# Backward attention in groups of eight units: the query gradient's products three units later, the row jobs in units 2 to 4, the key and value sums in units 5 and 6, nine E buffers

## The chip, the cores and the metric

The kernel runs on one core of one Trainium2 chip. The metric is the device time of one execution in microseconds (us). The kernel before has a median of 1660.38 us over 3 runs (1658.82 to 1664.07). One execution was also profiled; its durations are those used below.

## The reference

One transformer block with a parallel sum, forward and backward, for one sequence of S = 2048 rows and D = 448 columns, H = 16 heads of 28, and a feed-forward width of F = 1792, all in bfloat16:

```
xn  = (x - mean(x)) / sqrt(var(x) + 1e-5)
qkv = xn @ wqkv                     # split into q, k, v; 16 heads of 28
p   = softmax(q @ k.T * 28**-0.5)
out = x + (p @ v) @ wo + (silu(xn @ w_gate) * (xn @ w_up)) @ w_down
```

The outputs are `out` and the gradients, for a given `grad_out`, of `x`, `wqkv`, `wo`, `w_gate`, `w_up` and `w_down`.

## The kernel before

Every engine has its own queue and works through it in the order in which the program issues. The order is written out by hand (`tc.manual_schedule()`); waits between engines are put in automatically from which tile an instruction reads or writes. A tile pool with n buffers hands them out in turn, so a new tile waits until the last reader of the tile n places before it has ended.

**Forward, to about 750 us.** Normalisation, projections, the forward attention, the whole feed-forward part and its weight gradients run interleaved. This part isn't touched.

**Backward attention, about 750 to 1573 us.** Heads are worked in 8 pairs (`pr`). For each pair there are 4 chunks of 512 keys (`kc`), 2 windows of 1024 queries (`w`) and in each window 8 tiles of 128 queries (`qi`). One (pr, kc, w, qi) is a *unit*: 128 queries by 512 keys for two heads. There are 512 units. Eight units with the same pr, kc and w form a *group* W (64 groups, `UW = 8`); k is the unit's number and `pos = k % 8` its place in the group.

In the loop's turn k (L845 to L910) are issued, in this order:

- PE: the score product S(k), two matmuls into an `sd` tile (L858).
- PE: the product D(k-1) of the output gradient with the values, two matmuls into the next `sd` tile (L868).
- ACT: E(k) = exp of S(k) into an `E` tile (L877).
- DVE: ds(k-1) = D(k-1) times E(k-1) (L885). Two units share one `ds` tile.
- SP: after units 1, 3 and 5 of a group, a transposing DMA of the two ds into the group's `dsT` tile (L887).
- PE: one piece of other work, depending on pos.

The `sd` pool has 3 buffers of two banks each. The pool `ps_x` has one buffer, named `aux`, which the row jobs and the query gradient use in turn. `ps_acc` has one, named `acc`.

The other work by pos, for group W:

| pos | piece |
|---|---|
| 7, 0, 1 | the row job's matmuls in three parts ("fillers"; a job runs over from pos 7 of one group to pos 1 of the next) |
| 2 | `job_out`: ACT copies the job's result (`row_o`, L747, or `dwq_raw`, L711), a POOL DMA stores it. `pe_transpose`: PE transposes the last two ds of group W-1 into an `sd` tile (L794), ACT copies one half to `dsT` and then DVE the other (L796) |
| 3 | `acc_mm` of the last three units of group W-1 |
| 4, 5 | `dq_mm`: the query gradient's products of group W-1, a half each (L809) |
| 6 | `dq_out`: DVE adds `aux` to the sum `dq_acc` or makes `dq_o` (L821, L824, L827). `acc_mm` of the first five units of group W |

`acc_mm` (L758) adds a unit's four matmuls to the sum of key and value gradients `acc` (L768). A sum runs over 16 units, two groups; after the last, ACT moves it out as `dkv_o` (L774) and, three turns later, SP transposes it (L781) and POOL stores it.

The jobs, one per group, are of three kinds: "y", 16 of them, makes rows of the output (19 matmuls, L732 and L734); "dx", 32, makes rows of the gradient through the feed-forward part (14 matmuls, L738); "dwq", 12, makes a gradient of `wqkv` (16 steps of four short matmuls, L700 and L702). Job W's data (`ck`) are loaded at the start of group W-2. Group 17 and the groups after 61 have none.

**End, to 1658 us.** The last parts of the `wqkv` gradient and the gradient of `x`. This part isn't touched.

Of the kernel before, what the change touches and what calls it, by code (L numbers as in the profile page):

```python
# [37 lines left out]
def kernel(  # L38
# [405 lines left out]
    for fc in range(NFC):  # L444
        nxt = dW_items(fc)
        for sc in range(4):
            k = (len(pend) + 3 - sc) // (4 - sc)
# [185 lines left out]
    ast = ExitStack()  # L633
    ckp = ast.enter_context(tc.tile_pool(name="ckp", bufs=3))
    spg_.append(ast.enter_context(tc.tile_pool(name="spg", bufs=2)))
    ework = ast.enter_context(tc.tile_pool(name="ework", bufs=8))
    dwork = ast.enter_context(tc.tile_pool(name="dwork", bufs=5))
    twin = ast.enter_context(tc.tile_pool(name="twin", bufs=2))
    dqa = ast.enter_context(tc.tile_pool(name="dqa", bufs=1))
# [2 lines left out]
    UW = 8  # L642
    units = [(pr, kc, w, qi) for pr in range(NPR) for kc in range(4) for w in range(2) for qi in range(UW)]
    N = len(units)
    NW = N // UW
# [27 lines left out]
    jobs = {i + 1: j for i, j in enumerate(order) if j}  # L673
# [16 lines left out]
    def dwq_mms(g, c, ps):  # L690

        out = []
        lhs = lambda t: xn_sp[:, t, c * P:(c + 1) * P]
        for t in range(NT):
            w, s_, cb = t // 8, t % 8 // 4, t % 4

            def f(t=t, w=w, s_=s_, cb=cb):
                for hp in range(2):
                    kv, dq = dsp[2 * g + hp]
                    pe.matmul(ps[:, hp * P:(hp + 1) * P], lhsT=lhs(t), rhs=kv[:, t, :],  # L700
                              start=(t == 0 and hp == 0), stop=(t == NT - 1), skip_group_check=True)
                    pe.matmul(ps[:, 256 + hp * 64:256 + hp * 64 + 64], lhsT=lhs(t),  # L702
                              rhs=dq[:, w, cb, s_, :],
                              start=False, stop=(t == NT - 1), skip_group_check=True)
            out.append(f)
        return out
# [16 lines left out]
    def job_mms(i, ps):  # L723
        j = jobs[i]
        if j[0] == "dwq":
            return dwq_mms(j[1], j[2], ps)
        if j[0] == "y":
            t, x = chunk[i]
            out = []
            for n in range(NFC + G):  # L730
                rhs = (wtile["wd"][:, n, :] if n < NFC else wo_pad[:, n - NFC, :D])
                out.append(lambda n=n, rhs=rhs: pe.matmul(ps[:, :D], lhsT=t[:, n, :], rhs=rhs,  # L732
                                                          start=(n == 0), stop=False))
            out.append(lambda: pe.matmul(ps[:, :D], lhsT=ident_bf[:], rhs=x[:], start=False, stop=True))  # L734
            return out
        t = chunk[i]
        w = wtile[("wg", "wu")[j[1]]]
        return [lambda n=n: pe.matmul(ps[:, :D], lhsT=t[:, n, :], rhs=w[:, n, :],  # L738
                                      start=(n == 0), stop=(n == NFC - 1)) for n in range(NFC)]
# [13 lines left out]
    E, DS, st = {}, {}, {}  # L753
# [44 lines left out]
    def dq_mm(W, half):  # L798
        pr, kc, w, _ = units[W * UW]
        g, hp = pr // 2, pr % 2  # L800
        Ks, dsT = spt[g, 1], st[("dsT", W)]
        if half == 0:
            st["dq"] = ps_x.tile([P, 512], FP32, name="aux")
        ps = st["dq"]
        for kt in range(2 * half, 2 * half + 2):
            for s_ in range(2):
                for j in range(2):
                    r = 64 * s_ + HP * j
                    pe.matmul(ps[r:r + HP, :], lhsT=Ks[:, kc * 4 + kt, 64 * hp + HP * j:64 * hp + HP * j + HP],  # L809
                              rhs=dsT[:, 4 * s_:4 * s_ + 4, j, kt, :], start=(kt == 0), stop=(kt == 3),  # L810
                              tile_position=(0, r), skip_group_check=True)

    def dq_out(W):
        pr, kc, w, _ = units[W * UW]
        g, hp = pr // 2, pr % 2
        ps = st["dq"]
        if (pr, w) not in dqacc:
            dqacc[(pr, w)] = dqa.tile([P, 512], FP32, name=f"dq_acc{w}")
        acc = dqacc[(pr, w)]
        if kc == 0:  # L820
            dve.tensor_scalar(out=acc[:], in0=ps[:], scalar1=SCALE, scalar2=None, op0=ALU.mult)  # L821
            return
        if kc < 3:
            dve.scalar_tensor_tensor(out=acc[:], in0=ps[:], scalar=SCALE, in1=acc[:], op0=ALU.mult, op1=ALU.add)  # L824
            return
        o = outp.tile([P, 512], BF16, name="dq_o")
        dve.scalar_tensor_tensor(out=o[:], in0=ps[:], scalar=SCALE, in1=acc[:], op0=ALU.mult, op1=ALU.add)  # L827
        dq = dsp[pr][1]

        def later():  # L830
            sp.dma_start_transpose(out=dq[:, w].rearrange("p c s r -> p c (s r)"), in_=o[:])
            for s_ in range(2):
                k0 = 4 * w + 2 * s_
                pool.dma_start(
                    out=dqkv_d[k0:k0 + 2, 64 * hp:64 * hp + 64, g, :].rearrange("k p s -> p k s"),
                    in_=o[64 * s_:64 * s_ + 64, :].rearrange("p (k s) -> p k s", k=2))
        sp_later.append((k_now[0] + 1, later))
# [4 lines left out]
    job_load(1)  # L842
    job_load(2)
    fillers = []
    for k in range(N + UW):  # L845
        W, pos = k // UW, k % UW
        k_now[0] = k
        if k < N:
            pr, kc, w, qi = units[k]
            if pos == 0:  # L850
                job_load(W + 2)
            if pos == 4:
                extra_load(W)
            q, kv = qd[pr]
            qt = 8 * w + qi
            s_ps = ps_sd.tile([P, 2, 512], FP32, name="sd")
            for j in range(2):
                pe.matmul(s_ps[:, j, :], lhsT=q[HP * j:HP * j + HP, qt * P:(qt + 1) * P],  # L858
                          rhs=kv[HP * j:HP * j + HP, kc * 512:(kc + 1) * 512],
                          start=True, stop=True, tile_position=(HP * j, 0))  # L860
        if 1 <= k <= N:
            pr, kc, w, qi = units[k - 1]
            q, kv = qd[pr]
            qt = 8 * w + qi
            d_ps = ps_sd.tile([P, 2, 512], FP32, name="sd")
            for j in range(2):
                r = 64 + HP * j
                pe.matmul(d_ps[:, j, :], lhsT=q[r:r + HP, qt * P:(qt + 1) * P],  # L868
                          rhs=kv[r:r + HP, kc * 512:(kc + 1) * 512],
                          start=True, stop=True, tile_position=(r, 0))  # L870
        if pos == 2 and W in jobs:
            job_out(W, st["job"])
        if pos == 6 and W >= 1:
            dq_out(W - 1)
        if k < N:
            E[k] = ework.tile([P, 2, 512], BF16, name="E")
            act.activation(out=E[k][:], in_=s_ps[:], func=ACT.Exp, scale=SCALE)  # L877
        if 1 <= k <= N:
            u = k - 1
            if qi == 0:  # L880
                st[("dsT", u // UW)] = twin.tile([P, UW, 2, 4, P], BF16, name="dsT")
            if u % 2 == 0:
                DS[u // 2] = dwork.tile([P, 2, 2, 512], BF16, name="ds")
            ds = DS[u // 2]
            dve.tensor_tensor(out=ds[:, u % 2], in0=d_ps[:], in1=E[u][:], op=ALU.mult)  # L885
            if qi in (1, 3, 5):
                sp.dma_start_transpose(  # L887
                    out=st[("dsT", u // UW)][:, qi - 1:qi + 1].rearrange("p u j c q -> p (u j c) q"),
                    in_=ds[:].rearrange("p u j c -> p (u j c)"))
        while sp_later and sp_later[0][0] <= k:  # L890
            sp_later.pop(0)[1]()

        if pos == 7 and W + 1 in jobs:
            st["job"] = ps_x.tile([P, 512], FP32, name="aux")
            fillers = job_mms(W + 1, st["job"])
        if pos in (7, 0, 1):
            n = -(-len(fillers) // (3 - (pos + 1) % UW))
            for f in fillers[:n]:
                f()
            fillers = fillers[n:]  # L900
        if pos == 2 and W >= 1:
            pe_transpose(W - 1)
        if pos == 3:
            for u in range(max(k - 6, 0), k - 3):
                acc_mm(u)
        if pos in (4, 5) and W >= 1:
            dq_mm(W - 1, pos - 4)
        if pos == 6:
            for u in range(k - 6, min(k - 1, N)):
                acc_mm(u)  # L910
    while sp_later:
        sp_later.pop(0)[1]()
    ast.close()
# [90 lines left out]
```

## Time and profile before

| what | us |
|---|---|
| median of the runs | 1660.38 |
| the profiled execution | 1660.34 |
| its span | 1658.3 |
| forward and feed-forward part | 0 to 750 |
| groups 1 to 62 of the backward part | 775.5 to 1549.3 |
| PE busy in 775 to 1560 | 728.2 of 785 |
| DVE busy in 775 to 1560 | 667.9 of 785 |
| ACT busy in 775 to 1560 | 604.0 of 785 |

The profile names an instruction by its line, engine, operation and tiles (`out<-in`), with its number, its busy time and its mean duration in ns. "Idle before" is time in which the engine stood still in front of that instruction, with what ended the wait. PE's matmuls overlap, so its busy share isn't a share of its peak; PEld is the loading of weights. The clock is the share of full speed that PE was granted.

### The profile page before, as it was taken

How to read it: one execution, taken by the hardware profiler on the slowest of the kernel's cores; microseconds unless marked ns; L12 is line 12 of the kernel's file. 1: busy time of each engine (PE TensorE's matmuls, PEld its weight loads, DVE VectorE, ACT ScalarE, POOL GpSimd, SP SyncE). 2: the span in 40 equal slices, each digit the busy share in tenths (PEclk: the TensorE clock that was granted, in tenths of full speed). 3: DMA queues.
4: the chain of work that ended last, by engine and by line, in shares of the span. 5: the costliest groups of instructions: out<-in, count | busy, mean ns of one | idle time of the engine just before them, and what ended most of it. 6: DMA issues, size and time to landing. Idle time of an engine off the chain costs nothing.

```text
span 1658.3 us, 31281 instructions
## 1 busy us (share of the span) xinstructions
PE 1490.9 (90%) x12176; PEld 569.2 (34%) x12176; DVE 1135.6 (68%) x1479; ACT 1180.5 (71%) x1268; POOL 241.7 (15%) x449
## 2 busy tenths in 40 slices
PE   3799999999899999896988989999999999999784
PEld 1233333333233333222333335333335334433352
DVE  6365556665455455535877889878888889898635
ACT  3588888887777667674767778767787788878511
POOL 4001111111101111111111012111112011111132
PEclk8799999999988999897999999999999999999888
DMA  4576648675665567649999999999999999999862
GB/s 138 108 152 137 142 92 160 130 139 120 132 123 121 113 132 149 135 89 221 215 227 216 223 191 188 214 207 216 197 205 201 205 225 191 192 200 189 154 223 88
DMA packets 761300, 277.66 MB, mean 167 GB/s; under 512 B 729280, under 2 KB 740512, under 8 KB 761152
## 3 DMA queue, kind: packets, MB, share of 16 engines
q1 hardware_dynamic: 744736, 238.61, 74.5%
q0 software_dynamic: 15008, 36.75, 8.2%
q8 instruction: 95, 1.56, 0.4%
q10 hardware_dynamic: 1408, 0.30, 0.1%
q14 instruction: 53, 0.43, 0.1%
HBM read 64.15 MB, written 59.24 MB: 74 GB/s over the span
## 4 chain that ended last, share of the span: by engine, by line
PE 67%; DMA 13%; DVE 7%; ACT 6%; issue 4%; SPq 1%; POOL 1%; ACTq 0%; POOLq 0%; DVEq 0%
PE s_ps L600 9%; PE f_ps L389 8%; PE f_ps L363 8%; PE sd L858 7%; DMA dsT<-ds 7%; PE aux L738 5%; PE acc L768 5%; PE o_ps L577 4%; PE aux L809 4%; PE sd L868 3%; PE aux L732 3%; PE f_ps L168 3%; ACT dsT L796 3%; DMA f_sp<-hduT 3%; PE sd L794 2%
## 5 line engine op out<-in xcount | busy, mean ns | idle before, releaser
L885 DVE TENSOR_TENSOR ds<-sd,E 128x1024 bf16<-128x1024 f32 x512 | 609.5, 1218 | 80.5 <-PE sd L868 39.8
L877 ACT ACTIVATE E<-sd 128x1024 bf16<-128x1024 f32 x512 | 523.1, 1028 | 189.6 <-PE sd L868 129.1
L604 ACT ACTIVATE eT<-s_ps 128x1024 bf16<-128x1024 f32 x512 | 519.7, 1025 | 170.7 <-PE s_ps L600 164.7
L858 PE MATMUL sd<-KV,QD 32*128 32x512 bf16 x1024 | 204.6, 394 | 37.3 <-DVE dsT L796 19.4
L868 PE MATMUL sd<-KV,QD 32*128 32x512 bf16 x1024 | 205.2, 391 | 10.6 <-ACT E L877 6.8
L600 PE MATMUL s_ps<-qT,kT 32*128 32x512 bf16 x1024 | 203.8, 400 | 4.8 <-DVE qT L177 3.2
L389 PE MATMUL f_ps<-xnT,wgu 128*128 128x512 bf16 x448 | 132.3, 395 | 8.8 <-DMA wgu<-in_B_w_up_dram 8.2
L768 PE MATMUL acc<-E,dOsp 128*32 128x512 bf16 x1024 | 138.4, 393 | 0.1
L768 PE MATMUL acc<-ds,Qsp 128*32 128x512 bf16 x1024 | 138.2, 393 | 0.0
L858 PEld LDWEIGHTS <-QD 32*128 32x128 bf16 x1024 | 60.2, 91 | 218.3 <-issue 208.6
L600 PEld LDWEIGHTS <-kT 32*128 32x128 bf16 x1024 | 48.1, 91 | 205.6 <-issue 198.8
L809 PE MATMUL aux<-dsT,Ksp 128*32 128x512 bf16 x1024 | 94.0, 407 | 21.3 <-DMA dsT<-ds 21.1
L363 PE MATMUL f_ps<-xn_sp,f_sp 128*128 128x448 bf16 x448 | 111.4, 361 | 0.0
L577 PE MATMUL o_ps<-eT,v_sp 128*32 128x512 bf16 x1024 | 101.6, 398 | 0.9 <-DMA v_sp<-vT 0.9
L738 PE MATMUL aux<-W,ck 128*128 128x448 bf16 x448 | 101.6, 355 | 0.0
L868 PEld LDWEIGHTS <-QD 32*128 32x128 bf16 x1024 | 76.9, 91 | 65.0 <-issue 52.2
L401 DVE SCALAR_TENSOR_TENSOR g<-t_sb,f_ps 128x512 f32<-128x512 f32 x56 | 38.4, 686 | 67.0 <-ACT t_sb L399 67.0
L363 PEld LDWEIGHTS <-f_sp 128*128 128x128 bf16 x672 | 52.5, 99 | 82.9 <-issue 44.4
L796 DVE COPY dsT<-sd 128x1024 bf16<-128x1024 bf16 x64 | 44.3, 692 | 52.7 <-ACT dsT L796 52.7
L794 PE MATMUL sd<-ident_bf,ds 128*128 128x128 bf16 x1024 | 69.8, 222 | 3.2 <-DVE ds L885 2.5
L796 ACT COPY dsT<-sd 128x1024 bf16<-128x1024 bf16 x64 | 64.9, 1014 | 10.6 <-PE sd L794 6.3
L389 PE MATMUL f_ps<-dyT,wdT 128*128 128x512 bf16 x224 | 70.6, 400 | 0.8 <-DMA dyT<-dy_sp 0.8
(129 smaller groups left out, 1696.8 us busy)
## 6 DMA issues: line engine op xcount, KB each, us to landing
ck<-hO_d SPq DMA_DIRECT2D x17, 576.0 KB, 4.7
hO_d<-hduT SPq DMA_DIRECT2D x56, 128.0 KB, 3.2
da_d<-hduT SPq DMA_DIRECT2D x56, 128.0 KB, 3.0
du_d<-hduT SPq DMA_DIRECT2D x56, 128.0 KB, 3.1
ck<-da_d SPq DMA_DIRECT2D x16, 448.0 KB, 4.5
ck<-du_d SPq DMA_DIRECT2D x16, 448.0 KB, 4.5
dq_c<-dqkv_d SPq DMA_DIRECT2D x8, 768.0 KB, 4.4
dqkv_d<-dkv_o POOLq DMA_DIRECT2D x64, 64.0 KB, 4.1
```

The costliest lines, as they stand in the source:

```text
L363: pe.matmul(acc[:, :D], lhsT=src[:, t, wi, :], rhs=rhs[:, t, :D], start=(t == 0), stop=(t == NT - 1))
L389: pe.matmul(st[name][:], lhsT=w(c), rhs=src[:, tsl, c, :], start=(c == 0), stop=(c == 3))
L577: pe.matmul(o_ps[HP * hh:HP * (hh + 1), :], lhsT=v[:, kt, HP * hh:HP * (hh + 1)], rhs=e[hh // 2][:, hh % 2, :], start=(kt == 0), stop=(kt ...
L600: pe.matmul(s_ps[:, j, :], lhsT=kT[r:r + HP, kt * P:(kt + 1) * P], rhs=qT[r:r + HP, qc * 512:(qc + 1) * 512], start=True, stop=True, tile_ ...
L604: act.activation(out=e[:], in_=s_ps[:], func=ACT.Exp, scale=SCALE)
L738: return [lambda n=n: pe.matmul(ps[:, :D], lhsT=t[:, n, :], rhs=w[:, n, :], start=(n == 0), stop=(n == NFC - 1)) for n in range(NFC)]
L768: pe.matmul(acc[r:r + HP, :], lhsT=src[:, qt, 64 * hp + HP * j:64 * hp + HP * j + HP], rhs=m[:, j, :], start=(qt == 0), stop=(qt == NT - 1 ...
L809: pe.matmul(ps[r:r + HP, :], lhsT=Ks[:, kc * 4 + kt, 64 * hp + HP * j:64 * hp + HP * j + HP], rhs=dsT[:, 4 * s_:4 * s_ + 4, j, kt, :], sta ...
L858: pe.matmul(s_ps[:, j, :], lhsT=q[HP * j:HP * j + HP, qt * P:(qt + 1) * P], rhs=kv[HP * j:HP * j + HP, kc * 512:(kc + 1) * 512], start=Tru ...
L868: pe.matmul(d_ps[:, j, :], lhsT=q[r:r + HP, qt * P:(qt + 1) * P], rhs=kv[r:r + HP, kc * 512:(kc + 1) * 512], start=True, stop=True, tile_p ...
L877: act.activation(out=E[k][:], in_=s_ps[:], func=ACT.Exp, scale=SCALE)
L885: dve.tensor_tensor(out=ds[:, u % 2], in0=d_ps[:], in1=E[u][:], op=ALU.mult)
```

## The change

The pieces of other work change places in the group. Each query gradient half moves three turns later, from pos 4 and 5 to pos 7 and to pos 0 of the next group; its sum follows at pos 1. The transposes move from pos 2 to pos 1. The job of group W now lies wholly in group W, at pos 2, 3 and 4, and its result is copied at pos 5. The sums of the three late units move from pos 3 to pos 5, those of the five others stay at pos 6. The loop has two turns more, and the E pool one buffer more. No instruction is added or taken away.

```diff
-    ework = ast.enter_context(tc.tile_pool(name="ework", bufs=8))
+    ework = ast.enter_context(tc.tile_pool(name="ework", bufs=9))
...
-    for k in range(N + UW):
+    for k in range(N + UW + 2):
...
-        if pos == 2 and W in jobs:
+        if pos == 5 and W in jobs:
             job_out(W, st["job"])
-        if pos == 6 and W >= 1:
-            dq_out(W - 1)
+        if pos == 1 and W >= 2:
+            dq_out(W - 2)
...
-        if pos == 7 and W + 1 in jobs:
+        if pos == 2 and W in jobs:
             st["job"] = ps_x.tile([P, 512], FP32, name="aux")
-            fillers = job_mms(W + 1, st["job"])
-        if pos in (7, 0, 1):
-            n = -(-len(fillers) // (3 - (pos + 1) % UW))
+            fillers = job_mms(W, st["job"])
+        if pos in (2, 3, 4):
+            n = -(-len(fillers) // (5 - pos))
             for f in fillers[:n]:
                 f()
             fillers = fillers[n:]
-        if pos == 2 and W >= 1:
+        if pos == 1 and 1 <= W <= NW:
             pe_transpose(W - 1)
-        if pos == 3:
-            for u in range(max(k - 6, 0), k - 3):
+        if pos == 5:
+            for u in range(max(k - 8, 0), min(k - 5, N)):
                 acc_mm(u)
-        if pos in (4, 5) and W >= 1:
-            dq_mm(W - 1, pos - 4)
         if pos == 6:
-            for u in range(k - 6, min(k - 1, N)):
+            for u in range(min(k - 6, N), min(k - 1, N)):
                 acc_mm(u)
+        if pos == 7 and W >= 1:
+            dq_mm(W - 1, 0)
+        if pos == 0 and W >= 2:
+            dq_mm(W - 2, 1)
```

## The prediction

> **What bounds the kernel now.** I read the page first, then the waits of the backward stage, then a table of stretches, and last the timeline of one group of eight units. From the page:
>
> ```profile
> span 1658.3 us, 31281 instructions
> PE 1490.9 (90%) x12176; PEld 569.2 (34%) x12176; DVE 1135.6 (68%) x1479; ACT 1180.5 (71%) x1268; POOL 241.7 (15%) x449
> L885 DVE TENSOR_TENSOR ds<-sd,E 128x1024 bf16<-128x1024 f32 x512 | 609.5, 1218 | 80.5 <-PE sd L868 39.8
> L877 ACT ACTIVATE E<-sd 128x1024 bf16<-128x1024 f32 x512 | 523.1, 1028 | 189.6 <-PE sd L868 129.1
> ```
>
> The groups touched by the change run from 775.5 to 1549.3 us (groups 1 to 62): 773.8 us, 12.48 each. The waits from 775 to 1560 us name two losses that the change could reach:
>
> ```profile
> DVE dsT L796 <- ACT dsT L796: 50.9, 63, 1.9
> PE aux L809 <- DMA dsT<-ds: 20.2, 20, 1.9
> PE sd L858 <- DVE dsT L796: 19.4, 62, 0.6
> PE sd L868 <- ACT E L877: 6.5, 30, 0.6
> ```
>
> The query gradient's products (L809) waited in 20 of 62 groups for the transposed ds to land. Stretches of a late group, a plain "dx" group, a "y" group, a "dwq" group (PE, PEld, DVE, ACT, POOL busy; clock; DMA):
>
> ```profile
> 1185.80:1200.30 14.50, 12.73 (x113) 4.46 (x113) 10.87 (x11) 9.50 (x11) 0.59 (x1) 0.88 1.05 180
> 1213.00:1224.75 11.75, 11.43 (x111) 4.44 (x111) 10.32 (x11) 9.44 (x11) 0.59 (x1) 1.00 1.10 201
> 800.10:812.40 12.30, 11.81 (x120) 4.82 (x119) 10.69 (x11) 9.44 (x10) 0.59 (x1) 1.00 0.98 216
> 1407.10:1418.80 11.70, 11.18 (x162) 6.23 (x160) 10.52 (x11) 9.45 (x10) 1.80 (x7) 1.00 0.99 179
> ```
>
> Groups that don't wait for DMA repeat to 0.1 us: 11.75 (dx), 11.76 (dwq), 12.29 (y). Late ones take up to 15.5, partly because the clock falls (0.88 above); DMA is full in all of them. So an undisturbed group is a fixed dance of PE, ACT and DVE, in which PE is nearly full but pauses for buffers. Its steps, from the timeline of 1213.0 to 1224.75:
>
> ```profile
> 1214.50 0.39 PE L858 MATMUL sd<-KV,QD 32*128 32x512 bf16 x2
> 1214.93 1.02 ACT L877 ACTIVATE E<-sd 128x1024 bf16<-128x1024 f32 x1 [0.48 <-PE sd L868]
> 1216.33 1.07 PE L794 MATMUL sd<-ident_bf,ds 128*128 128x128 bf16 x16
> 1217.43 1.01 ACT L796 COPY dsT<-sd 128x1024 bf16<-128x1024 bf16 x1
> 1218.48 0.69 DVE L796 COPY dsT<-sd 128x1024 bf16<-128x1024 bf16 x1 [0.75 <-ACT dsT L796]
> 1219.22 0.39 PE L858 MATMUL sd<-KV,QD 32*128 32x512 bf16 x2 [0.29 <-DVE dsT L796]
> ```
>
> **Constants** from that group: score product S to its exponential E, 0.43; E 1.03, the next ACT job starts 0.10 before its end; D (L868) to its DVE product ds, 0.50; ds 1.21, next DVE job 0.08 before its end; D to the next PE job 0.32; that job to the next S: 5 job matmuls 1.05, 4 0.86, transposes T 1.03, three acc units 0.76, five 1.19, half of dq 0.58. A buffer is taken 0.05 after its reader ends. The three sd buffers go round: D(k) takes S(k)'s buffer (needs E(k)), S(k) takes D(k-3)'s. T shifts the round once: T needs the buffer of the second D before it, the next D that of the D right before T, the S after that T's own.
>
> **Part 1: dq three units later.** Before, the products come 7.2 us after the last ds that their DMA carries (in the quiet group that ds ends at 1224.3, the products start at 1231.5); late DMAs came up to 1.9 us after that. In the walk below it is 12.3 us (11.52 to 23.87). All 20 waits go. What they cost: y groups at 12.29, the others at 11.75 or their own quiet length (11.56, 11.88, 12.52 for groups 16, 17, 62) give 737.7 us; 773.8 - 737.7 = **-36.1**. Of it 20.2 is waiting; the rest is lower clock and re-start. Bounds: 20 and 36; I take 36, since of groups 1 to 61 every one with a clock below 0.95 also has the DMA wait.
>
> **Part 2: the new order, walked for a dx group.** Units 0 to 7, S0 at 0. Unit 7 of the group before holds only half a dq, so S0 follows S7 by 0.91, and E7 ends at 0.55: D7 0.60, dq 0.92, S1 1.50. ds7 1.10 to 2.31. E0 0.45 to 1.48, D0 1.53. T needs ds7: 2.36 (PE could at 1.85, pause **0.51**). S2 3.39. DVE: dq_acc (L824, now between ds7 and ds0) 2.23 to 2.91, ds0 2.83 to 4.04. D1 needs D0's buffer, hence ds0: 4.09 instead of 3.40, pause **0.69**. The ACT copy of T 3.46 to 4.48, the DVE copy 4.51 to 5.20: it no longer holds S3 (5.46). Job: 4.41, S3 5.46, S4 6.84, D3 6.97, S5 8.15, D4 8.35. ACT: E4 ends 8.30, row_o (L747) 8.30 to 8.83, E5 8.73 to 9.76. Three acc units 8.67, S6 9.43, D5 waits for E5: 9.81 (pause 0.33), five acc units 10.13, S7 11.32, next S0 12.23. So **12.23 against 11.75, +0.48**: the 0.8 us DVE idle at the copy shrinks, but PE pays with the chain E7, D7, ds7, dq_acc, ds0, D1. The same walk with 7, 6 and 6 job matmuls (y; 1.44, 1.25, 1.25): **13.04 against 12.29, +0.75**. With dwq (1.13, 0.96, 0.96): **12.36 against 11.76, +0.60**. A group without a job: 11.4. Bounds for dx: 0.27 (rival 1) and 0.68 (four of the links 0.05 longer); I keep the walk, since the same constants give the old group back at 11.75.
>
> **Part 3: acc in units 5 and 6.** Every second group ends a sum; its evacuation dkv_o (L774, 0.69) stood three units ahead of the next sum, now one: ACT runs it at 9.66 to 10.35, the five acc units start at 10.40, not 10.13: **+0.27 in 31 groups, +8.4**. Bounds 0 (if hidden) and 31 x 0.69 = 21; I take the walk.
>
> **Moved past or free.** The ninth E buffer: with it E5 and E6 find buffers freed by earlier sums; no instruction. On SP, the dkv_sp transpose (median landing 3.4) goes behind the next ck load (issue 0.5), and dq_sp behind one dsT transpose: free, since the dwq job that reads them comes over a group later; the last ones lie under the final dsT landing. Job loads gain three units before use. POOL's stores move with their sources; POOL is 15% busy. Start: the first job leaves group 0 (-1.0). Tail: one dq half and its DVE sum run before the last DMA lands (+0.3; 0 to 1).
>
> **Sum.** y 16 x 13.04 = 208.6; dx 32 x 12.23 = 391.4; dwq 12 x 12.36 = 148.3; groups 17 and 62 11.4 + 12.5; dkv_o 8.4: 780.6 against 773.8, +6.8. With start and tail +6.1. The profiled execution took 1660.34 us (span 1658.3), the median is 1660.38, so **1666**.
>
> **The clock.** The late group above: 14.43 long, 1.45 of DMA wait, clock 0.88; 14.43 - 11.75 - 1.45 = 1.2 us is the price of a fall. My new pauses are 0.3 to 0.7 each, and groups with pauses of 0.2 to 0.4 ran at 1.00, so I count none. The Trainium skill ("TensorE: Matmul & The Clock Gate", section "Why this matters for your kernels") puts the limit at idle gaps of about 3 us; the trace does not agree, as the clock fell at 1.45. The same page's "A second HAM failure mode: psum-queue depth-cycling" says that frequent short idles between bursts can make the clock oscillate; by that rule the sum would be 1741, rival 4's.
>
> **Rivals.**
> 1. *Faster: D1 doesn't wait for ds0.* The decisive point is whether dq_acc and ds0 end before PE has issued S2 (3.39). If so, D1 comes at 3.40 and S3 is held by the DVE copy alone (5.25): 0.21 less in 60 groups, 13 us: **1653**. For: DVE has 1.4 us free in a quiet group. Against: before, D2 (1217.78) follows the end of ds1 (1217.73) in just this place, without a dq_acc ahead.
> 2. *The dkv_o evacuation is hidden*: 8 less, **1658**, no change. Against: ACT has E5 and E6 on both sides of it.
> 3. *The DMA lateness returns three units later*, because the DMA queues are full (q1 at 100.9% of 16 engines in the stage) and the lag grows: half the gain gone, **1684**. Against: runs of 10 quiet groups (47 to 57) show no growing lag.
> 4. *The clock falls in every group*: 62 x 1.2 = 75: **1741**. For: units 7, 0 and 1 are light one after the other, then transposes. Against: groups 17 to 21, with PE pauses of 0.4 to 2.2, kept 1.00.
>
> **Chances.** My sum 0.52 (1660 to 1675 on its own), rival 1 0.20, rival 2 0.10, rival 3 0.13, rival 4 0.05. The range leaves out rival 4 and half of the tails of 1 and 3: 1650 to 1684. Faster or slower by over 0.3% (5 us, about what a measurement tells from nothing): rival 1 and the low tail of my sum give faster 0.22; rival 2 and the sum's part below 1665 give same 0.22; the rest, 0.56, slower.
>
> **What would show it.** Right: the wait of L809 for DMA gone and clock 1.00 throughout; quiet dx groups near 12.2 and y near 13.0; L868 waiting for DVE ds some 0.6 per group; L768 waiting for ACT dkv_o 31 times; the DVE copy's wait for ACT's far below 50.9. Wrong: dx groups at 11.9 or less (rival 1), L809 still waiting for DMA (3), clock below 0.95 in quiet groups (4).

## The result

| | median us | lowest to highest | runs |
|---|---|---|---|
| before | 1655.04 | 1646.84 to 1664.07 | 20 |
| after | 1664.26 | 1660.71 to 1672.39 | 20 |

The kernel after takes 1.0058 times as long (95% interval 1.0043 to 1.0074), 9.2 us more. The forecast was 1666 us and slower by 6. Its profiled execution took 1663.57 us, with a span of 1661.8.

The page of the kernel after, the lines that answer to those of before:

```profile
span 1661.8 us, 31231 instructions
PE 1464.9 (88%) x12176; PEld 556.9 (34%) x12176; DVE 1146.1 (69%) x1479; ACT 1179.5 (71%) x1268; POOL 242.0 (15%) x449
L885 DVE TENSOR_TENSOR ds<-sd,E 128x1024 bf16<-128x1024 f32 x512 | 619.6, 1221 | 101.1 <-PE sd L868 75.0
L877 ACT ACTIVATE E<-sd 128x1024 bf16<-128x1024 f32 x512 | 517.5, 1025 | 170.7 <-PE sd L868 134.8
```

PE is busy for 26 us less than before, yet the span is 3.5 us longer. The same matmuls ran at a higher mean clock (0.962, before 0.950), but PE stood still more. The waits of the kernel after in the backward part (775 to 1565 us; each line: who waited for whom, us in total, times, longest):

```profile
PE sd L794 <- DVE ds L885: 29.1, 61, 0.8
DVE dsT L796 <- ACT dsT L796: 28.5, 62, 0.5
PE sd L868 <- DVE ds L885: 22.0, 62, 0.4
PE sd L868 <- ACT E L877: 15.1, 62, 0.2
PE acc L768 <- ACT dkv_o L774: 5.9, 31, 0.2
DVE ds L885 <- DMA dsT<-ds: 4.1, 3, 1.9
PE aux L809 <- DMA dsT<-ds: 0.7, 1, 0.7
```

Two exchanges are to be seen. The 20.2 us in which L809 waited for DMA are down to 0.7. In their place stand two waits for DVE that come once in every group: the transposes (L794) for the last ds of the group before, and D (L868) for the first ds of this one. The sum of keys and values waits for `dkv_o` 31 times, in every second group.

The stretches of five groups: a dx group, the next dx group with its `dkv_o`, a y group, a dwq group, and group 62, which has no job (columns as in the table of before: PE, PEld, DVE, ACT, POOL busy; clock; DMA):

```profile
1204.61:1216.82 12.21, 11.14 (x114) 4.30 (x112) 10.94 (x11) 9.40 (x11) 0.59 (x1) 1.00 1.12 228
1216.82:1229.28 12.46, 11.20 (x114) 4.41 (x111) 10.80 (x11) 9.86 (x12) 1.79 (x3) 1.00 1.02 208
795.33:808.36 13.03, 11.83 (x120) 4.61 (x117) 10.90 (x11) 9.39 (x11) 0.59 (x1) 1.00 1.11 215
1402.79:1415.16 12.37, 11.16 (x164) 5.88 (x161) 10.80 (x11) 9.33 (x11) 1.80 (x7) 1.00 1.02 173
1538.84:1552.58 13.74, 11.08 (x101) 3.61 (x98) 10.80 (x11) 9.58 (x11) 1.20 (x2) 0.75 0.80 145
```

The walk of the prediction said 12.23, 12.50, 13.04 and 12.36 for the first four. PE's timeline of the first of them (start, duration, line, and in brackets the idle time ahead and its releaser) shows the chain:

```profile
1204.61 0.39 PE L858 MATMUL sd<-KV,QD 32*128 32x512 bf16 x2
...
1207.02 1.05 PE L794 MATMUL sd<-ident_bf,ds 128*128 128x128 bf16 x16 [0.47 <-DVE ds L885]
1208.01 0.39 PE L858 MATMUL sd<-KV,QD 32*128 32x512 bf16 x2
1208.75 0.39 PE L868 MATMUL sd<-KV,QD 32*128 32x512 bf16 x2 [0.35 <-DVE ds L885]
1209.07 1.12 PE L738 MATMUL aux<-W,ck 128*128 128x448 bf16 x5
1210.13 0.39 PE L858 MATMUL sd<-KV,QD 32*128 32x512 bf16 x2
```

From S0 on: T at 2.41 (walked 2.36), D1 at 4.14 (4.09), the job at 4.46 (4.41), the next score product, S3 of the walk, at 5.52 (5.46). The profile gives D1's wait as 0.35 and not the walked 0.69, because it counts from the modelled end of the matmul before (1208.40); the instant is the same.

### The profile page after: what moved, and what is told of

The parts are those of the page before. It is cut to its first block, busy times and chain, and to the rows that moved or that the text cites. A ratio compares the mean times of both kernels' runs of the same rounds, so it can differ in the third digit from the quotient of the medians.

```text
span 1661.8 us, 31231 instructions
## 1 busy us (share of the span) xinstructions
PE 1464.9 (88%) x12176; PEld 556.9 (34%) x12176; DVE 1146.1 (69%) x1479; ACT 1179.5 (71%) x1268; POOL 242.0 (15%) x449
## 4 chain that ended last, share of the span: by engine, by line
PE 60%; DVE 17%; ACT 8%; DMA 6%; issue 5%; SPq 1%; POOL 1%; DVEq 0%; ACTq 0%; POOLq 0%
DVE ds L885 10%; PE s_ps L600 9%; PE f_ps L363 8%; PE f_ps L389 8%; ACT E L877 6%; PE acc L768 6%; PE sd L868 4%; PE o_ps L577 4%; PE sd L858 4%; PE aux L738 4%; PE aux L732 4%; PE f_ps L168 3%; DVE dq_acc L824 1%; ACT dkv_o L774 1%; DMA f_sp<-hduT 1%
## 5 line engine op out<-in xcount | busy, mean ns | idle before, releaser
L885 DVE TENSOR_TENSOR ds<-sd,E 128x1024 bf16<-128x1024 f32 x512 | 619.6, 1221 | 101.1 <-PE sd L868 75.0
L877 ACT ACTIVATE E<-sd 128x1024 bf16<-128x1024 f32 x512 | 517.5, 1025 | 170.7 <-PE sd L868 134.8
L868 PE MATMUL sd<-KV,QD 32*128 32x512 bf16 x1024 | 202.6, 386 | 43.6 <-DVE ds L885 23.5
L858 PE MATMUL sd<-KV,QD 32*128 32x512 bf16 x1024 | 201.3, 390 | 15.5 <-ACT E L877 9.5
L858 PEld LDWEIGHTS <-QD 32*128 32x128 bf16 x1024 | 49.3, 91 | 192.2 <-issue 182.8
L868 PEld LDWEIGHTS <-QD 32*128 32x128 bf16 x1024 | 74.8, 91 | 108.6 <-issue 102.2
L794 PE MATMUL sd<-ident_bf,ds 128*128 128x128 bf16 x1024 | 67.6, 219 | 30.1 <-DVE ds L885 30.0
L809 PE MATMUL aux<-dsT,Ksp 128*32 128x512 bf16 x1024 | 79.3, 384 | 1.6 <-DVE dsT L796 0.9
L794 PEld LDWEIGHTS <-ds 128*128 128x128 bf16 x1024 | 62.1, 97 | 43.6 <-issue 42.4
```

Of the source, the lines that this page charges most:

```text
L794: pe.transpose(ps[:, u, i, :], ds[:, u, i // 4, (i % 4) * P:(i % 4 + 1) * P], ident_bf[:])
```

## Experiments

The lateness of before (36.1 us of the forecast) and the price of the new order (42.2, so that 6.1 remain) were each far larger than their difference. Theory: both are real and nearly cancel. Rival: both are small. The experiments take each term by itself, then test its links. The kernel before ran beside every experiment (medians of 1656.8 to 1657.3 us); the kernel after ran beside it in the result alone (1655.04), so a difference of 2 us to after says nothing.

**1. Take away what delays the transposing DMAs.** Loads for the next pair stand in the same SP queue as these DMAs. Both kernels were run without these loads (37 DMAs, not the 34 that the expectation names), so that later pairs work on the first pair's tiles:

```diff
-        if 1 <= r <= 4 and pr + 1 < NPR:
-            load_pair(pr + 1, [r - 1])
+        if r == 1 and pr + 1 < NPR:
+            qd[pr + 1] = qd[pr]
         elif r >= 5 and pr % 2 == 0 and pr + 2 < NPR:
-            load_rows(pr // 2 + 1, r - 5)
+            spt[pr // 2 + 1, r - 5] = spt[pr // 2, r - 5]
```

> The kernel before without the loads of the next pair and of the next rows during the backward groups (every pair works on the data of the first, so the gradients are not the reference's); no instruction of PE, ACT or DVE and no place in any queue changes but for 34 DMAs left out on SP. Theory (these loads hold the transposing DMAs up, and what that costs is 30 to 36 us): the waits of L809 for DMA go, the groups are quiet at 11.75 and 12.29, 1622 to 1628. Rival (late DMAs are one execution's accident, or cost nothing): 1648 or more.

> The changed kernel without the same loads (the gradients are not the reference's). Theory (the change has already taken nearly all of the lateness away): only 1 to 5 us less than the changed kernel, 1658 to 1663, so that without the loads the change costs 34 to 42 us, near the 44 that the walk of the order gave. Rival (the loads weigh on both orders alike): 30 us less, as in the kernel before.

Before without the loads: 1629.07 us (1615.91 to 1635.02), beside 1657.3 for before on the same chip; ratio 0.9814 (0.9782 to 0.9846). After without them: 1663.92 (1661.01 to 1667.23), ratio to before 1.0046 (1.0028 to 1.0063). The waits of before without the loads, 765 to 1540 us:

```profile
PE aux L809 <- DMA dsT<-ds: 4.4, 5, 2.0
```

and of after without them, 765 to 1560 us:

```profile
PE sd L794 <- DVE ds L885: 29.9, 63, 0.8
PE sd L868 <- DVE ds L885: 22.0, 62, 0.4
PE acc L768 <- ACT dkv_o L774: 5.8, 31, 0.2
```

Both times lie just above their expected ranges. So 28 of the 36 us of lateness come from these loads, and what is left waits five times. Groups 1 to 62 of before then took 745.2 us, 7.5 more than the 737.7 of the prediction's quiet groups: the loads and the rest make up the 36. The kernel after doesn't notice the loads. With them gone, the new order costs 1663.92 - 1629.07 = 34.9 us; with the 7.5 that before still loses, that is the 42 of the forecast. Both terms are real, and the rival is out.

Where the lag arises is to be seen on SP, which works through its DMAs in order. The first line is of before, with the shortest, the median and the longest time in ns for which one transposing DMA holds SP. The others are SP's timeline in the kernel after, in one of its few late groups:

```profile
L887 SPq DMA_TRANSPOSE dsT<-ds x189: 1364/3077/5748, 774.1 to 1559.2; - x189
```

```profile
1094.47 1.26 SPq L831 DMA_TRANSPOSE dq_sp<-dq_o  x1
1095.78 1.16 SPq L549 DMA_DIRECT2D QD<-qT_d  x1
1097.04 5.25 SPq L887 DMA_TRANSPOSE dsT<-ds  x2
```

SP's DMAs together hold it for 11.6 us per group in before (groups 2 to 60) and for 10.2 without the loads; a quiet dx group lasts 11.75. That isn't waiting for ds: in 146 of 180 cases in before the ds was done when SP came to its DMA, which then held SP for 3.2 us (median). So SP has hardly any time left, and falls behind. In before it starts a transposing DMA 1.55 us after its ds has ended (median), without the loads 0.18, and in the kernel after 2.46. From start to landing these DMAs take much the same in all three: 5.6, 5.3 and 5.4. In the stretch shown, the group's last ds that goes by DMA ended at 1091.4, SP came to its DMA (the second of the last line) at 1100.2, and the products waited 0.7 us for it. So the lag is longer in the kernel after than in before, and is covered by the later place of the products. Why one transposing DMA holds SP for 3 us isn't shown.

**2. Only the later query gradient, without the new order.** The products of `dq` come one whole group later, at their old place in it. For that, `dsT` is cut into two half tiles (3 and 2 buffers); memory for them comes from `dq_o` and `dkv_o`, which get one buffer each instead of two.

```diff
-        if pos in (4, 5) and W >= 1:
-            dq_mm(W - 1, pos - 4)
+        if pos in (4, 5) and W >= 2:
+            dq_mm(W - 2, pos - 4)
...
-        if pos == 6 and W >= 1:
-            dq_out(W - 1)
+        if pos == 6 and W >= 2:
+            dq_out(W - 2)
...
-        o = outp.tile([P, 512], BF16, name="dq_o")
+        o = outp1.tile([P, 512], BF16, name="dq_o")
```

> The kernel before with one part of the change alone: the query gradient's products and their sum stay at pos 4, 5 and 6 but belong to the group one earlier still, so they come eight units later after the transposing DMA (the dsT tile is split in two halves, three and two buffers, and dq_o and dkv_o get one buffer each to make room). Nothing else of the order changes. Theory (late DMA, with the fall of the clock that it brings, costs the kernel before 30 to 36 us, and slack alone takes it away): all groups quiet at 11.75 (dx) and 12.29 (y), no wait of L809 for DMA, 1655 - 31 + some 5 for the wqkv jobs that now wait for dq_sp and for the tail = 1622 to 1635. Rival (the DMA queues are full, so the lag moves to another wait): 1648 or more.

1672.04 us (1669.44 to 1679.6), ratio 1.0102 (1.0064 to 1.014): missed by some 40 us. Its waits, 775 to 1575 us:

```profile
PE aux L704 <- DMA dq_sp<-dq_o: 14.0, 2, 7.5
DVE dq_o L829 <- DMA dq_sp<-dq_o: 12.2, 4, 3.8
DVE ds L885 <- DMA dsT<-ds: 11.9, 12, 2.3
```

The products no longer wait for DMA, and quiet groups take the old 11.75. But the edit made three new waits: for the only `dq_o` buffer, for `dq_sp` in the dwq jobs (which now read it too early: groups of 20.3 and 21.4 us), and for `ds` buffers that a late DMA is still reading.

**3. The same, mended.** Two `dq_o` buffers (the memory comes from `x_c`; `dkv_o` still has one), and the dwq jobs of the first and third batch come two groups later (the first is shown).

```diff
-            x = ckp.tile([P, D], BF16, name="x_c")
+            x = ckp2.tile([P, D], BF16, name="x_c")
...
-    order = [("y", t) for t in range(NT)] + [None] + [("dwq", 0, c) for c in range(4)]
-    order += [("dx", 0, t) for t in range(NT)] + [("dwq", 1, c) for c in range(4)]
+    order = [("y", t) for t in range(NT)] + [None] + [("dx", 0, t) for t in range(2)]
+    order += [("dwq", 0, c) for c in range(4)] + [("dx", 0, t) for t in range(2, NT)]
+    order += [("dwq", 1, c) for c in range(4)]
```

> The kernel before with the query gradient's products eight units later, without the three faults of the first try: dq_o keeps two buffers (x_c has two instead of three for it), and the dwq jobs of pairs 0, 1 and 4, 5 come two jobs later, so that dq_sp has landed. Theory: the first try's waits for dq_sp go (12 us of DVE and 14 of PE, with clock falls some 36), quiet groups at 11.75 and 12.29, some 10 us of waits of ds for the transposing DMA stay: 1634 to 1640. Rival (the lag of the DMA queues only moves to the next wait): 1650 or more.

1647.79 us (1641.95 to 1656.75), ratio 0.9951 (0.9927 to 0.9974). It beats both kernels, but by 8 us less than expected: between the theory and the rival. Its waits, 765 to 1545 us:

```profile
DVE ds L887 <- DMA dsT<-ds: 27.2, 21, 2.7
PE acc L772 <- DVE ds L887: 15.6, 14, 2.0
```

The lag didn't go away. Once the products came late enough, the next user of the same DMAs met it: the `ds` pool has five buffers, and a new `ds` waits until the DMA has read the old one. In the kernel after this wait came only 3 times (4.1 us).

**4. The link dq_acc in front of ds0.** In the kernel after, the sum of `dq` goes behind the product ds of unit 0.

```diff
-        if pos == 1 and W >= 2:
-            dq_out(W - 2)
         if k < N:
             E[k] = ework.tile([P, 2, 512], BF16, name="E")
...
+        if pos == 1 and W >= 2:
+            dq_out(W - 2)
         while sp_later and sp_later[0][0] <= k:
```

> The changed kernel with the query gradient's sum issued on DVE behind the product of unit 0 instead of ahead of it. Theory (the chain D7, ds7, dq_acc, ds0, D1 holds PE): D1 comes at 3.49 instead of 4.09 in the group, the job then waits for the sum to leave aux (4.09 instead of 4.41), and S3 is held by the DVE copy at 5.25 instead of 5.46: dx 0.21, y 0.32, dwq 0.29 less, together 15 us: 1649. Rival (the loss comes from the two light units side by side, not from the sum's place): within 3 us of 1664.

1658.22 us (1653.57 to 1667.56); 6 less than after, where 15 were expected. y groups (12.69 for 13.03) and dwq groups (12.07 for 12.37) shrank as expected, dx groups by 0.1 only. PE's timeline of a dx group:

```profile
1204.93 0.39 PE L858 MATMUL sd<-KV,QD 32*128 32x512 bf16 x2
1205.08 0.39 PE L868 MATMUL sd<-KV,QD 32*128 32x512 bf16 x2
1205.67 1.11 PE L738 MATMUL aux<-W,ck 128*128 128x448 bf16 x5 [0.20 <-DVE dq_acc L821]
1206.82 0.39 PE L858 MATMUL sd<-KV,QD 32*128 32x512 bf16 x2
```

D1 comes without a wait, 0.60 earlier in the group than in the kernel after. But now the job waits: it writes `aux`, which has one buffer, and the sum of `dq` is still reading it. The job gains 0.33, and S3 0.24. The group then falls back in step at D2, at 5.48 where it was at 5.52 (D2 needs E2, which ACT runs behind its copy of T). And lateness came back (waits of 760 to 1545 us):

```profile
DVE ds L883 <- DMA dsT<-ds: 17.5, 18, 2.1
PE aux L809 <- DMA dsT<-ds: 1.1, 1, 1.1
```

**5. Half of dq before the five sums.** In the kernel after, pos 6 and 7 exchange their pieces, so that unit 7's place is full again and `dkv_o` gets more room.

```diff
-        if pos == 6:
-            for u in range(min(k - 6, N), min(k - 1, N)):
-                acc_mm(u)
-        if pos == 7 and W >= 1:
+        if pos == 6 and W >= 1:
             dq_mm(W - 1, 0)
+        if pos == 7:
+            for u in range(min(k - 7, N), min(k - 2, N)):
+                acc_mm(u)
```

> The changed kernel with the five sums and the first half of the query gradient's products exchanged: products at pos 6, sums at pos 7, so that the two light units are no longer side by side and E7 runs under the sums. Theory (the chain begins with E7, which the light unit 7 leaves exposed): D7 comes 0.37 earlier in a dx group and 0.5 in a y group; odd dx groups 11.86 instead of 12.23; in even groups dkv_o now delays E6 and costs 0.39 instead of 0.27. Together 19 us less: 1645. Rival (the chain begins at the sum on DVE, E7 has slack): under 5 us.

1655.78 us (1649.07 to 1667.35), ratio to before 1.0002 (0.9975 to 1.003); 8.5 less than after, where 19 were expected. Quiet dx groups are 11.91 and 12.23 long, as walked (11.86 and 12.25). The wait of T for ds7 is gone (29.1 to 0.3), the one of D1 stays. The rest was lost to lateness (760 to 1540 us):

```profile
PE sd L868 <- DVE ds L885: 20.4, 61, 0.4
PE aux L809 <- DMA dsT<-ds: 8.2, 8, 1.5
DVE ds L885 <- DMA dsT<-ds: 3.6, 4, 1.9
```

**6. Both edits, with and without the loads** (edits 4 and 5 together; edit 1 in the second).

> The kernel after with both edits: the sum of dq behind the product ds of unit 0, and pos 6 and 7 exchanged (half of dq at 6, five acc units at 7). Each alone took 6 and 8.5 us off the kernel after (1664.3) where the walk gave 15 and 20, because late transposes of ds came back. By the walk both together shorten a quiet dx group to about 11.6 to 11.9 (after: 12.20 odd, 12.46 even), y to about 12.2 to 12.7, dwq to about 11.6 to 12.1: 30 to 36 us, 1628 to 1634 without lateness. Theory (the shorter the group, the more of the lag of the DMA queues shows, as in the kernel before, where it costs 28): 1655 to 1660, no better than either edit alone. Rival (the measured gains add up): 1650. Second rival (the lag is a thing of the old place of dq alone, and the two single edits were held by something else): 1628 to 1636.

> The same with the loads of the next pair's tiles left out (every pair works on the data of the first, so the gradients of wqkv and x are not the reference's; the instructions of PE, DVE and ACT are the same). Theory: the lateness goes as it did in the kernel before (1657 to 1629) and the quiet groups are left, 1630 to 1636, some 25 us below the version with loads. Rival (the edits were held by something else than the loads): within 8 us of the version with loads.

1658.16 us (1651.67 to 1663.05) with the loads, as the theory said, and 1642.56 (1637.2 to 1648.37) without them, 7 above the expected range. The loads cost this order 15.6 us: about nothing in the kernel after, 28 in the kernel before. But the quiet groups were misjudged: they take 11.90 and 12.23, no less than in run 5. The waits of the version with loads, 760 to 1545 us, and a stretch of its PE timeline:

```profile
PE aux L809 <- DMA dsT<-ds: 10.7, 11, 2.5
DVE ds L883 <- DMA dsT<-ds: 6.6, 5, 2.0
PE sd L868 <- DVE ds L883: 2.6, 3, 1.7
```

```profile
1228.30 0.39 PE L868 MATMUL sd<-KV,QD 32*128 32x512 bf16 x2
1228.90 1.10 PE L738 MATMUL aux<-W,ck 128*128 128x448 bf16 x5 [0.21 <-DVE dq_acc L824]
```

D1's wait for ds0 is gone (20.4 to 2.6), and the job's wait for `dq_acc` and `aux` has taken its place at the same instant: S3 stands at 4.91 in the group, in run 5 at 4.92.

**7. Double the sum of dq.** A second DVE operation of the same size goes ahead of `dq_out` in the kernel after; its result is not used.

```diff
         if pos == 1 and W >= 2:
+            extra = outp.tile([P, 512], BF16, name="extra")
+            dve.tensor_scalar(out=extra[:], in0=st["dq"][:], scalar1=SCALE, scalar2=None, op0=ALU.mult)
             dq_out(W - 2)
```

> The changed kernel with a second DVE instruction of the same size ahead of the query gradient's sum at pos 1, into a scratch tile. Theory (every us between ds7 and ds0 on DVE is on PE's path): 0.60 per group, 37 us: 1701. Rival (DVE has 0.5 us idle before its copy and takes it up): under 10 us.

1725.71 us (1724.62 to 1726.7): +61 to after, not +37. Two neighbouring dx groups in one table of stretches:

```profile
1058.15:1071.21 13.06, 11.20 (x115) 4.42 (x112) 11.40 (x12) 9.86 (x12) 1.79 (x3) 1.00 1.00 218
1071.21:1085.53 14.32, 12.65 (x116) 4.50 (x113) 11.40 (x12) 9.33 (x11) 0.59 (x1) 0.88 1.10 212
```

The first is 0.60 longer than its like in the kernel after (12.46), as are y (13.62 for 13.03) and dwq groups (13.23 for 12.63): the sum of `dq` lies on the path with its full length. The second should take 12.20 + 0.60 = 12.80; it has a clock of 0.88 and takes 1.5 more, as do 14 other dx groups, nearly every second one. PE's timeline in it:

```profile
1075.94 0.39 PE L868 MATMUL sd<-KV,QD 32*128 32x512 bf16 x2 [0.95 <-DVE ds L887]
1076.27 2.01 PE L738 MATMUL aux<-W,ck 128*128 128x448 bf16 x5
```

After the pause of 0.95, five job matmuls take 2.01; in the kernel after they take 1.12.

**8. Eight E buffers in the new order.**

```diff
-    ework = ast.enter_context(tc.tile_pool(name="ework", bufs=9))
+    ework = ast.enter_context(tc.tile_pool(name="ework", bufs=8))
```

> The changed kernel with eight E buffers, as before. Theory: E5 must wait for the first of the three sums of pos 5 (ends 9.07 in the dx group), starts at 9.10 instead of 8.74, and with it D5, the five sums and the next group: 0.37 in 46 groups, 0.24 in 16, 21 us: 1685. Rival (E has slack at this place): under 5 us.

1685.73 us (1682.48 to 1689.28): +21.5 to after, as expected. A dx group takes 12.61 and 12.87 instead of 12.21 and 12.46. The waits, 765 to 1590 us:

```profile
PE sd L868 <- ACT E L877: 37.6, 124, 0.7
ACT E L877 <- PE acc L768: 14.1, 37, 1.2
```

An exponential must wait until the sums of the three late units, issued two turns later than before, have read an old E, and D waits for the exponential. So the ninth buffer is what makes the new order's late sums free.

## Why the prediction was right

**The sum.** The touched part of the profiled execution, from the start of each group:

| term | predicted | measured |
|---|---|---|
| 16 y groups, with `dkv_o` in 8 | 210.8 | 211.1 |
| 32 dx groups, with `dkv_o` in 16 | 395.7 | 396.1 |
| 12 dwq groups, with `dkv_o` in 6 | 149.9 | 149.9 |
| groups 17 and 62, with `dkv_o` in 62 | 24.2 | 26.7 |
| start (group 0) | -1.0 | -1.9 (21.1 for 23.0) |
| after group 62 | +0.3 | +0.2 (109.2 for 109.0) |

**Part 1, the lateness.** Right in its mechanism: of 20 waits of the products, one is left. Its size of 36.1 rests on the difference between late and quiet groups (the lengths that it lists add up to 737.3, not 737.7, which matters little); the loads account for 28 of it (experiment 1), and 4.4 us of waits remain without them. What the prediction left out is that the lag is only hidden by this order and not removed: runs 3 to 6 met it again as soon as the group was shorter, or the next reader (`ds`) had fewer buffers to spare. That is rival 3's mechanism. It is at work in the kernel after too, where SP lags by 2.46 us against 1.55 (experiment 1); but the products come 12.7 us after their last ds (median; walked 12.3, in before 7.4), and 4.8 us of such waits are left in all. The longer a group, the more time SP has: its lag (median) is 0.2 us in run 7, whose quiet dx groups take 12.80 and 13.06, 1.3 in run 8 (12.61 and 12.87), 2.5 in the kernel after (12.21 and 12.46), 3.7 in run 4 (12.11 and 12.38), and 3.1 and 3.0 in runs 5 and 6 (11.91 and 12.23). Run 4 stands out of the row, and each edit moved something else too; that the length alone does it is argued.

**Part 2, the walk.** Right step by step, to 0.06 us. Runs 4, 5 and 7 show each link: ds7 in front of T, `dq_acc` in front of ds0 (+0.60 for one more operation of its kind), ds0 in front of D1. *Rival 1* (D1 doesn't wait) is out: 62 waits. Even where D1 was freed, the gain was smaller than its 13 us, since the job then waits for `aux`.

**Part 3.** `dkv_o` costs 0.25 in 31 groups (predicted 0.27), and *rival 2* is out.

**The step that was mis-sized** is the one of the groups without a job: 12.95 and 13.74 instead of 11.4 and 12.5 (+0.27 in 62). The clock fell to 0.87 and 0.75 there. This is rival 4's mechanism, in 2 groups instead of 62; all others but the first two ran at 1.00. It isn't the new order's alone. Group 17 ran at 1.00 in before (11.88) but at 0.87 in before without the loads (12.69). Group 62 ran at 0.73 in before already (12.52), and the forecast took that length over; why it takes 1.2 more in the kernel after stays open. The prediction had counted the clock as safe because groups 17 to 21 of before kept 1.00 with "PE pauses of 0.4 to 2.2"; these are sums over a group, and the longest single pause was 0.64. By the rule of the Trainium skill ("TensorE: Matmul & The Clock Gate", "A second HAM failure mode: psum-queue depth-cycling") frequent short idles would make it oscillate; the trace of after does not agree, with three pauses of 0.24 to 0.47 in each dx group at 1.00, while run 7, with a pause of 0.95 among them, shows such a change of clock in nearly every second dx group.

**The median.** +8.3 us from the start of group 0 on, predicted +6.1. Yet the two profiled executions differ by 3.2 only, since the one of before started its group 0 at 752.5 and the one of after at 747.6, in a part that wasn't touched; ten other profiled executions of this study start it between 745 and 751.4. So before's profiled execution was about 5 us slow, as its median over 20 runs says too (1655.04 for 1660.34). That 1666 came so near to 1664.26 is in part luck: a sum that was 2 us short stood upon a base that was 5 us long.

## What to carry to other kernels

When a change hides a lag by moving its reader, ask who uses the same buffers next (`ds`, `dq_o` and `aux` here), since the wait moves on to them, and whether the queue that issues the DMAs has time left in a period. When it moves work across a rhythm of several engines, walk one undisturbed period with durations from the trace, and price the stages without filler work apart. Two large terms of opposite sign are best measured one at a time, by taking away the cause of one.

## What the runs showed of the hardware

- The clock fell to 0.88 in groups whose longest PE pause was 0.95 us, the others being 0.25 and 0.47 (run 7), and stayed at 1.00 in quiet groups of the kernel after with 0.24, 0.35 and 0.47. The Trainium skill ("TensorE: Matmul & The Clock Gate", "Why this matters for your kernels") puts the limit at about 3 us; the traces do not agree. In before the clock fell after a pause of 0.84 (group 29).
- The dx groups between the slow ones in run 7 had the same pause of 0.95 and kept 1.00. The clock records tell why. In all twelve traces the clock is either 1.00 or 0.50, and changes only on a grid of 3.41 us, whose place differs from execution to execution. Three steps of it in run 7, the first in a group at 1.00, the others in the next group (columns as before):

```profile
1059.27:1062.69 3.42, 2.19 (x30) 1.21 (x23) 3.41 (x4) 2.44 (x4) 0.00 (x0) 1.00 1.18 244
1072.93:1076.34 3.41, 1.99 (x25) 1.24 (x22) 3.41 (x5) 2.65 (x3) 0.00 (x0) 1.00 1.11 236
1076.34:1079.76 3.42, 3.42 (x12) 1.03 (x13) 2.08 (x3) 1.21 (x2) 0.00 (x0) 0.50 0.87 198
```

PE stood still for 1.23 us in the first and for 1.42 in the second, and a step at half clock followed the second alone. In groups 2 to 62 of run 7 all 19 steps that ended with a fall hold 1.42 to 1.79 us of standstill, the others at most 1.39. A dx group at 1.00 and the next at 0.88 take 13.06 + 14.27 = 27.33 us there, and eight steps of the grid 27.31: so the grid meets every second group at the same place. A threshold for other kernels isn't shown: in run 5 a step with 0.91 ended with a fall, in run 3 one with 1.72 did not.
- Leaving out 12 MB of loads (265.6 MB instead of 277.7 in a whole execution) took 28 us off the kernel before and about nothing off the one after. What the loads cost goes through SP's queue (11.6 us per group with them, 10.2 without), through a few transposing DMAs that came up to 1.9 us late (20 waits in before), and through the clock, which fell with them (0.88 in the late group shown of before). Of the 87 us that SP had less to do in all, 37 were the loads' own; for most of the rest, the transposing DMAs of ds held SP for less without them (529 us instead of 575).
